# Another emission order for a fused retention and gated MLP kernel

## The chip, the core and the metric

One NeuronCore of a Trainium2 chip runs the whole program in one launch. The metric is the device time in microseconds of that core. The kernel is written against five engines with a queue each: PE (TensorE), DVE (VectorE), ACT (ScalarE), POOL (GpSimd) and SP (SyncE, which here issues nearly all DMA transfers). An engine takes the instructions of its queue in the order in which the program emitted them.

## What is computed

Retention attention over 8 sequences of 576 positions with 8 heads of 64, then a gated MLP with a mix over the positions, and a residual:

```python
scores = (q @ k.T) / sqrt(64)
x = (scores * Dmat) @ v              # Dmat[i,j] = gamma_h**(i-j) for i >= j, else 0; heads side by side: (8, 576, 512)
h = gelu_tanh(x @ w_in)              # (8, 576, 1024)
u, w = h[..., :512], h[..., 512:]
w_n = (w - mean(w)) / sqrt(var(w) + 1e-6) * g_ln
w_s = einsum('ts,bsd->btd', w_sg, w_n) + b_sg[None, :, None]
out = x + (u * w_s) @ w_out
```

## The kernel before, in words

**Tiling.** The sequences go through in 4 pairs (p). A pair has 1152 positions, which are 9 tiles of 128 rows; the middle one is half of each sequence. The attention of a pair is done in 5 blocks (n = 0 to 4) of two tiles, but the middle one (n = 2) of one; block b is 5p + n, tile i is 9p + m. The MLP's position mix is done for each sequence ("batch", 2p + e).

**One block of attention.** SP loads q, k and v (`a_load`, lines 315 and 318). A preparation (`a_prep`) scales q and v by powers of gamma (line 361) and casts k (351; 349 on ACT); it is done by POOL, for block 0 by DVE and ACT too. q and k are transposed by PE (`a_T`, 398) and copied out by DVE (`a_Tev`, 413), or, from block 10 on, by a transposing DMA of SP (`a_TX`, 418). `a_S` (449) makes the scores, `a_Sev` on DVE masks them (462, 465). `a_Z` (485), `a_Zsum` (510, 513) and `a_Zev` (517, 519) keep the running state k.T v. `a_O` and `a_O2` (531) give the output, which ACT copies to the tile xT (`a_Oev`, 588).

**The MLP of a tile.** `m_V` (599) multiplies by the right half of w_in, ACT makes gelu of it (`m_Vg`, 606), DVE the statistics (`m_stats`, 614 and 615), POOL the reciprocal deviation (`m_rs`, four small instructions, 619 to 622) and ACT the normalised rows (`m_norm`, 634, 631). `m_U` (646) and `m_Ug` (656) do the left half. When the five tiles of a batch have been normalised, eight `m_W` (665) mix the positions, and `m_Wg` on DVE (675) gates. `m_O` (696; 691 adds x for the first pair) multiplies by w_out; `m_Oev` (711 on ACT for the first pair, 713 on DVE later, with the residual tile xr, which a transposing DMA, `m_X`, 705, makes from xT) writes the tile ob, and SP stores it (`m_store`, 718). The last tile, 35, is done in two halves.

**At the start.** Both halves of w_in come through two staging tiles (load at 239) and are cast by DVE (246) and ACT (248). Then the same staging tile of the right half takes four fifths of w_sg in two loads (260), so these wait for both casts. w_sg is cast (271), turned by `build_wT` (779) and copied (783). `to_col`, `col_math` and `to_rows` (724, 728 to 738, 745) make columns and rows of g_ln and b_sg; `rows` (749), `place_vmid` (767, 768) and `place_wT` (771, 772) put them into place. A fill (216) is a matmul on zeros that nothing reads; fill n is emitted by the name fn.

**Buffers.** Tiles are taken from rings by tag (`BUFS`): 8 of ld, 2 of ldq, 3 of vb, 2 each of qb, kb, qT and kT, 5 of xr, 4 of ob, 3 of vg. PSUM has a ring of two (pp: transposes, scores, attention outputs) and one of four (d: all the others, fills among them; an `a_Z` takes two, or one). The ring's next tile waits for the readers of the one that had its place.

**What sets the order.** The kernel first makes a list of 925 jobs, each with an engine and a function that emits its instructions; the job's number is its place in that list. `Planner.emit` then goes through the string `ORDER` and calls the functions in that order. Durations, due times and costs in `add(...)` are not used for it. So each engine's queue is the sub-list of its own jobs, in the order of `ORDER`, and the order of two jobs of different engines matters only through what they wait for and through the order in which tiles are taken from a ring.

The jobs that are spoken of by number:

| job | what |
|---|---|
| 0, 1, 2; 6, 7, 8; 12, 13, 14 | `a_load` of q, k, v of blocks 0; 1; 2 |
| 3, 9 | loads of w_in, right and left half |
| 4, 5 | casts of w_in's right half, DVE and ACT |
| 15, 16; 17 | loads of w_sg to the staging tile; its last rows |
| 23, 24, 25; 31, 32 | loads of q, k, v of block 3; k, v of block 4 |
| 72; 75; 76; 77, 79; 78, 80 | `zero_wnat`; `to_col`; `col_math`; `to_rows`; `rows` |
| 81, 82 | `place_vmid`, `place_wT` |
| 103, 104, 106, 107 | block 0: q prepared (DVE), k cast (ACT), `a_T`, `a_Tev` |
| 195, 197; 196, 198 | block 0: `a_S`; `a_Sev` |
| 267; 268, 270; 269, 271; 272, 273; 274, 275 | block 0: `a_Z`; `a_Zsum`; `a_Zev`; `a_O`, `a_O2`; `a_Oev` |
| 187, 188, 189, 190; 192, 193 | block 18: q twice, k, v prepared; block 19: k, v |
| 184; 775 | block 17: v prepared; `m_rs` of tiles 27 and 28 |
| 191, 194 | transposing loads of q, k of blocks 18 and 19 |
| 581, 585, 569, 577 | stores of tiles 15, 16, 13, 14 |
| 659, 667, 740 | `m_X` of tiles 18, 19, 23 |
| 907, 911, 915, 919, 922 | `m_O` of tiles 32, 33, 34, and of 35 in two halves |

Of the kernel before, what the change touches and what calls it, by code (L numbers as in the profile page):

```python
# [17 lines left out]
PR = dict(PB0=10000.0, O=4000.0, PB=9900.0, S=2000.0, S2=400.0, Z=1901.0, V=6000.0, V2=900.0, U=1260.0, W=4000.0, WS=19000.0, slack=60.0, pen=500.0)  # L18

ORDER = (  # L20
# [33 lines left out]
)  # L54


# [1006 lines left out]
```

## Time and profile before

| | |
|---|---|
| three runs | 214.28, 215.05 and 230.25 us |
| their median | 215.05 us |
| span of the profiled execution, first to last instruction | 212.7 us |
| busy in it: PE, DVE, ACT, POOL | 195.4, 147.3, 117.0, 118.4 us |
| mean granted TensorE clock | 0.991 |
| moved by DMA | 50.45 MB, 237 GB/s over the span |

A profile gives one execution; its span leaves out what lies before the first and behind the last instruction, and its time is not recorded apart from the span. In the rows, L and a number is a line of the kernel; "out<-in" are the tiles written and read; a bracket at the end tells how long the engine was idle ahead of the row and which engine's work ended that. SPq is SP issuing a DMA: a row of it is the time of the issue, not of the transfer. "Granted clock" is the share of full speed that TensorE's clock gate gave.

### The profile page before, as it was taken

To read this page: it belongs to the slowest core of one execution; us is meant where nothing else is said; L and a number is where in the kernel's file an instruction comes from. 1 tells how busy PE (TensorE), PEld (TensorE's weight loads), DVE (VectorE), ACT (ScalarE), POOL (GpSimd) and SP (SyncE) were. 2 spreads that over 40 slices of the span, in tenths; PEclk is the share of its full clock that TensorE was granted. 3 is DMA by queue.
4 is the path that set the end of the run, shared out by engine and by line. 5 is a ranking of instruction groups with operands and counts; after the bars stand their busy time and mean duration, and the time that the engine had idled before them with its cause. 6 is when DMAs were issued, how large, how long until landed. Compare 5 with 4: busy or idle time off the path is not lost.

```text
span 212.7 us, 7684 instructions
## 1 busy us (share of the span) xinstructions
PE 195.4 (92%) x3282; PEld 133.8 (63%) x3282; DVE 147.3 (69%) x287; ACT 117.0 (55%) x207; POOL 118.4 (56%) x169
## 2 busy tenths in 40 slices
PE   7796699788899999999999999899999899999992
PEld 5674585665656677765677666666475665666760
DVE  4783787767858489666857387687747686866473
ACT  5228757842785941888463867444642648443400
POOL 8955285979782999752868965008593344112000
PEclk9999969999999999999999999999999999999999
DMA  6999999999999999999999999999999897626755
GB/s 163 335 295 262 169 377 295 287 284 296 271 250 294 277 272 295 137 197 307 339 319 204 222 177 103 223 303 120 338 287 198 191 253 130 197 69 152 245 157 197
DMA packets 94228, 50.45 MB, mean 237 GB/s; under 512 B 45354, under 2 KB 87602, under 8 KB 94194
## 3 DMA queue, kind: packets, MB, share of 16 engines
q1 hardware_dynamic: 94176, 49.97, 101.1%
q8 instruction: 25, 0.41, 0.9%
q14 instruction: 9, 0.07, 0.1%
q10 hardware_dynamic: 18, 0.00, 0.0%
HBM read 32.79 MB, written 9.44 MB: 199 GB/s over the span
## 4 chain that ended last, share of the span: by engine, by line
PE 65%; DMA 14%; SPq 7%; POOL 5%; issue 3%; DVE 3%; ACT 2%; POOLq 0%; ACTq 0%
PE wp L665 16%; PE op L696 13%; PE hu L646 11%; PE hv L599 11%; DMA ld<-in_v_dram 7%; PE pp L531 5%; DMA ld<-in_k_dram 5%; SPq L315 4%; PE pp L449 3%; DMA kT<-kb 2%; POOL vb L361 2%; PE zp L485 2%; PE pp L398 2%; SPq L318 1%; POOL mv L620 1%
## 5 line engine op out<-in xcount | busy, mean ns | idle before, releaser
L361 POOL TENSOR_TENSOR vb<-ld,gpow 128x1024 bf16<-128x1024 f32 (+1 forms) x20 | 34.6, 1733 | 19.8 <-DMA out_dram<-ob 11.1
L462 DVE TENSOR_TENSOR ret<-pp,msk 128x1024 bf16<-128x1024 f32 x32 | 38.6, 1212 | 8.0 <-PE pp L449 7.9
L665 PE MATMUL wp<-wT,vn 128*128 128x288 bf16 x256 | 40.6, 286 | 0.0
L599 PE MATMUL hv<-w_in,xT 128*128 128x512 bf16 x144 | 36.6, 380 | 0.2 <-issue 0.2
L646 PE MATMUL hu<-xT,w_in 128*128 128x256 bf16 (+1 forms) x320 | 36.3, 262 | 0.3 <-DVE uT L675 0.3
L696 PE MATMUL op<-w_out,uT 128*128 128x512 bf16 (+1 forms) x148 | 35.7, 373 | 0.2 <-ACT vg L606 0.2
L614 DVE BATCH_NORM_STATS2 bst<-vg 128x6 f32<-128x512 f32 x36 | 24.6, 684 | 14.9 <-ACT vg L606 14.9
L606 ACT ACTIVATE vg<-hv 128x512 f32<-128x512 f32 x36 | 21.4, 596 | 23.8 <-PE hv L599 18.2
L646 PEld LDWEIGHTS <-w_in 128*128 128x128 bf16 x320 | 28.4, 98 | 7.4 <-issue 0.5
L675 DVE TENSOR_TENSOR uT<-wp,uT 128x288 bf16<-128x288 f32 x64 | 26.6, 448 | 8.1 <-PE wp L665 5.9
L634 ACT ACTIVATE vn<-vg,mv 128x512 bf16<-128x512 f32 x32 | 25.6, 810 | 11.5 <-POOL mv L622 11.3
L656 ACT ACTIVATE uT<-hu 128x512 bf16<-128x512 f32 x36 | 21.1, 593 | 19.3 <-PE hu L646 19.1
L665 PEld LDWEIGHTS <-vn 128*128 128x128 bf16 x256 | 24.1, 98 | 8.1
L361 POOL TENSOR_TENSOR qb<-ldq,gpow 128x1024 bf16<-128x1024 f32 x14 | 26.5, 1904 | 4.3 <-DMA ldq<-in_q_dram 3.8
L588 ACT ACTIVATE xT<-pp 128x512 bf16<-128x512 f32 (+1 forms) x40 | 20.4, 550 | 12.6 <-PE pp L531 12.4
L619 POOL TENSOR_SCALAR mv<-mv 128x2 f32<-128x2 f32 (+1 forms) x20 | 4.5, 226 | 37.0 <-DVE mv L615 25.9
L713 DVE TENSOR_TENSOR ob<-op,xr 128x512 f32<-128x512 f32 (+1 forms) x28 | 18.3, 668 | 9.2 <-PE op L696 7.4
L696 PEld LDWEIGHTS <-uT 128*128 128x128 bf16 x148 | 13.9, 98 | 11.9 <-issue 0.5
L599 PEld LDWEIGHTS <-xT 128*128 128x128 bf16 x144 | 12.8, 98 | 12.7 <-issue 0.5
L665 PE MATMUL wp<-wT,vmid 128*128 128x288 bf16 x64 | 18.4, 287 | 0.0
L351 POOL CAST kb<-ld 128x1024 bf16<-128x1024 f32 x14 | 14.5, 1038 | 3.8 <-DMA ld<-in_k_dram 3.8
L620 POOL TENSOR_TENSOR mv<-mv,mhalf 128x2 f32<-128x2 f32 (+1 forms) x20 | 13.8, 688 | 1.7
(100 smaller groups left out, 249.9 us busy)
## 6 DMA issues: line engine op xcount, KB each, us to landing
out_dram<-ob SPq DMA_DIRECT2D x35, 256.0 KB, 4.0
ld<-in_k_dram SPq DMA_DIRECT2D x16, 512.0 KB, 7.3
ld<-in_v_dram SPq DMA_DIRECT2D x16, 512.0 KB, 7.1
ldq<-in_q_dram SPq DMA_DIRECT2D x7, 1024.0 KB, 6.8
xT<-in_moe_w_sg_dram SPq DMA_DIRECT2D x2, 576.0 KB, 8.0
ld<-in_q_dram SPq DMA_DIRECT2D x2, 512.0 KB, 8.2
xT<-in_moe_w_in_dram SPq DMA_DIRECT2D x1, 1024.0 KB, 8.0
ld<-in_q_dram SPq DMA_DIRECT2D x8, 128.0 KB, 7.5
```

Of the source, the lines that this page charges most:

```text
L361: ve.tensor_tensor(dst, src, g.unsqueeze(len(src.shape) - 1).to_broadcast(list(src.shape)), op=Alu.mult)
L462: ins = nc.vector.tensor_tensor(ret[:].rearrange("p r (k t) -> p (r k) t", k=2), sc[:].rearrange("p r (k t) -> p (r k) t", k=2), (msk2 if ...
L588: nc.scalar.activation(dst, src, Act.Copy)
L599: ins = nc.tensor.matmul(hv[:], xTs[p][:, m, kk, :], w_in[:, kk, F2:], start=(kk == 0), stop=(kk == KK - 1))
L606: unfence(nc.scalar.activation(vgs[i][:], cur.pop(("hv", i))[:], Act.Gelu_apprx_tanh), ("V", i))
L614: nc.vector.bn_stats(bst[:], vgs[i][:])
L634: nc.scalar.activation(vn[:], vg[:], Act.Identity, scale=mv[:, s, 2:3], bias=mv[:, s, 3:4])
L646: ins = nc.tensor.matmul(hu[:, n, :], w_in[:, kk, 128 * c:128 * c + 128], xTs[p][:, m:m + w, kk, :], start=(kk == 0), stop=(kk == KK - 1), ...
L656: unfence(nc.scalar.activation(uTs[p][:, c0:c1, 128 * m:128 * m + 128 * w], cur.pop(("hu", i, half))[:], Act.Gelu_apprx_tanh), ("U", i, half))
L665: ins = nc.tensor.matmul(ps[:], vns[t0 + j][e][:, 128 * c:128 * c + 128], wT[e][j][:, half * HS:(half + 1) * HS], start=(j == 0), stop=(j ...
L675: ins = nc.vector.tensor_tensor(uTs[p][:, c, col:col + HS], cur.pop(("wp", b, c, half))[:], uTs[p][:, c, col:col + HS], op=Alu.mult)
L696: ins = nc.tensor.matmul(op[:], uTs[p][:, c, r], w_out[:, c, cs], start=(p >= XP and c == 0), stop=(c == KK - 1), skip_group_check=True)
```

## The change

The string `ORDER` is replaced by another with the same 925 jobs and the same six fills (4, 5, 6, 6, 10 and 14). Nothing else differs: every job emits the same instructions. The heads of the queues, before and after:

```
PE   before  f4 f6 75 f5 f6 77 79 106 267 197 195 f14 272 273
PE   after   f4 75 f10 f14 77 f6 106 197 195 f6 267 272 273 79
SP   before  0 1 2 3 6 7 8 12 17 16 15 13 14 23 9 24 31 25 34
SP   after   1 0 2 3 6 7 15 17 8 16 12 13 14 23 9 24 31 25 32
DVE  before  72 103 76 78 107 196 4 198 80 268 270 112
DVE  after   76 72 103 78 107 198 4 196 268 80 270 112
ACT  before  104 269 5 274 275 81 271 277 22
ACT  after   104 81 5 269 274 82 275 22 277
```

Of the later queues, a stretch of SP's and of POOL's, and the end of PE's:

```
SP   before  585 667 191 659 194 569 71 675 577 740 662
SP   after   191 194 581 585 569 659 740 667 577 71 662
POOL before  717 183 187 188 189 190 192 775 184 193 796
POOL after   183 187 188 775 190 184 189 192 796 811 193
PE   before  894 907 919 922 911 915
PE   after   904 907 911 915 919 922
```

The diff, cut to the lines that hold these places:

```diff
@@ -18,39 +18,39 @@
 ORDER = (
-    '0 f4 1 2 f6 72 3 73 6 103 75 74 f5 76 7 104 f6 77 79 105 78 106 8 107 267 197 269 195 f14 196 5 12 4 198 108 17 '
-    '80 272 16 268 270 109 273 274 15 13 275 111 81 276 112 279 110 14 201 199 271 277 113 22 289 278 f10 280 23 200 '
-    '21 20 290 202 291 19 9 281 18 24 293 114 82 292 91 286 89 92 294 116 90 31 101 117 87 83 115 287 102 97 88 93 '
-    '296 84 95 295 98 310 94 203 96 99 118 297 204 25 313 298 314 288 300 299 119 316 100 312 315 311 301 85 34 10 11 '
-    '122 302 317 120 123 282 32 318 307 320 86 319 303 36 321 124 308 322 126 304 283 33 305 127 309 121 323 205 207 '
-    '38 206 130 306 352 284 353 208 354 125 35 324 285 355 211 357 212 356 134 332 330 325 26 358 209 374 359 40 210 '
...
-    '781 665 711 657 700 712 579 780 666 583 717 256 713 580 187 719 185 658 581 782 584 718 66 765 186 714 188 70 '
-    '783 257 785 730 784 585 715 731 766 667 722 189 716 738 723 191 190 736 739 726 567 727 737 768 568 192 575 769 '
-    '771 576 767 668 659 772 663 770 194 660 669 775 773 569 258 71 664 792 774 661 184 675 794 793 577 802 795 799 '
-    '845 740 800 803 801 259 804 846 786 805 848 776 662 260 728 670 847 777 261 671 720 262 193 787 724 744 789 721 '
...
-    '910 887 892 898 888 893 891 838 889 918 904 839 899 905 840 896 900 902 897 901 894 903 914 907 895 919 908 922 '
-    '911 909 923 920 924 915 912 921 913 916 917 '
+    'f4 73 1 75 76 74 72 f10 f14 0 104 2 3 6 7 105 103 77 f6 106 78 107 197 195 198 4 81 5 15 17 8 108 109 110 16 '
+    '196 f6 267 268 269 272 273 79 274 80 270 111 276 82 275 22 277 f5 112 201 279 19 280 271 20 18 21 199 289 278 '
+    '202 281 290 291 200 292 93 85 86 94 12 13 14 23 286 113 114 87 293 97 98 88 294 101 102 95 116 117 96 115 9 118 '
+    '119 24 31 296 295 287 89 297 288 298 203 204 83 84 90 300 313 314 301 299 302 99 91 100 315 316 317 92 10 310 '
+    '122 311 307 11 318 120 124 123 319 322 282 320 305 308 309 283 312 126 303 127 306 321 304 323 25 32 33 205 284 '
+    '209 206 121 207 352 34 36 125 128 129 130 134 285 210 353 355 324 339 341 330 208 325 331 340 342 354 357 211 '
...
+    '253 182 183 185 579 738 767 254 186 739 770 580 782 257 187 188 775 69 66 190 68 70 184 189 192 783 583 567 584 '
...
+    '794 805 804 809 847 810 795 796 191 194 581 585 569 659 740 667 792 806 773 730 259 261 797 807 808 811 793 798 '
...
+    '842 843 747 906 914 751 918 898 910 836 844 892 888 889 893 896 894 899 897 895 900 902 903 901 904 905 907 908 '
+    '909 911 912 913 915 916 917 919 922 920 921 923 924 '
 )
```

44 rows, old and new, of the table ORDER are left out of this document.

## The prediction

> **What bounds the kernel now.** I read the page first, then the chain of waits, then the timeline of each queue for the first 60 us, because the two lists differ most there.
>
> ```profile
> span 212.7 us, 7684 instructions
> ...
> PE 195.4 (92%) x3282; PEld 133.8 (63%) x3282; DVE 147.3 (69%) x287; ACT 117.0 (55%) x207; POOL 118.4 (56%) x169
> ...
> GB/s 163 335 295 262 169 377 295 287 284 296 271 250 294 277 272 295 137 197 307 339 319 204 222 177 103 223 303 120 338 287 198 191 253 130 197 69 152 245 157 197
> ```
>
> TensorE is busy for 92% of the span, so after the start whatever it loses is lost at the end too. The transfers run at 250 to 380 GB/s in most of the first 16 slices (5.3 us each).
>
> ```profile
> 7.67 11.30 DMA ld<-in_v_dram
> ...
> 25.67 9.86 DMA ld<-in_k_dram
> 35.58 1.04 POOL kb L351
> ...
> 44.22 0.61 PE wp L665 x5
> ```
>
> The chain of waits (start, length, what) says who sets the pace of the start: two loads, 21 of the first 36 us, then a cast on POOL, and only from the first m_W at 44 us mostly TensorE. So there are two stages: loads until about 45 us, TensorE after it.
>
> ```profile
> 0.00:10.00 10.00, 7.83 (x64) 6.16 (x65) 6.08 (x30) 4.18 (x5) 8.66 (x32) 1.00 0.86 241
> 10.00:20.00 10.00, 8.30 (x190) 5.87 (x191) 6.51 (x8) 4.97 (x9) 5.11 (x4) 1.00 1.18 274
> 20.00:30.00 10.00, 7.22 (x140) 6.04 (x140) 7.32 (x15) 7.65 (x14) 5.08 (x9) 0.91 1.00 265
> 30.00:40.00 10.00, 9.88 (x178) 6.93 (x177) 7.43 (x16) 6.14 (x13) 7.54 (x10) 0.92 1.13 305
> 40.00:50.00 10.00, 7.31 (x201) 5.38 (x201) 6.67 (x8) 5.77 (x10) 8.18 (x8) 1.00 1.18 278
> ```
>
> By stretches (stretch, length, busy PE, PEld, DVE, ACT, POOL, granted clock, DMA share, GB/s): TensorE is idle for 9.5 of the 50 us, most of all at 20 to 30 and at 40 to 50, and the granted clock falls to 0.91 and 0.92 where TensorE was thin.
>
> **The change part by part.** No work is added or removed; every engine gets the same jobs in another order. I take the places where an order makes its engine wait.
>
> *The fills.* Ahead of the first transposes, a_T(0,q), TensorE had fills of 4, 6, 5 and 6; it now has 4, 10, 14 and 6, the 10 and 14 behind to_col and ahead of to_rows(0).
>
> ```profile
> 1.24 3.88 PE L216 MATMUL scr<-warm 128*128 128x256 f32 x10 [1.24 <-DVE warm L175]
> 6.03 0.20 PE L724 MATMUL tp<-identf,rsrc 9*128 9x9 f32 x1 [0.91 <-DMA rsrc<-in_moe_b_sg_dram]
> ...
> 8.74 0.66 PE L745 MATMUL tp<-ident,col 128*4 128x128 bf16 x9
> 9.33 0.64 PE L398 MATMUL pp<-ident,qb 64*128 64x64 bf16 x32
> ...
> 11.87 3.29 PE L216 MATMUL scr<-warm 128*128 128x256 f32 x14
> ```
>
> The fills of 10 and 14 are 24 records. At 11.87 one costs 0.235 us, at the start 0.388. All fast is 5.6 us, all slow 9.3. TensorE now idles from about 3 to 6.0 waiting for rsrc, so I take ten slow and 14 fast: 3.9 + 3.3 = 7.2, from 6.2 to 13.4. to_rows(0) (0.4 of the 0.66) and the six records of the next fill (1.4) follow: a_T(0,q) starts at 15.2 and not at 9.33, 5.9 later (4 to 8).
>
> *The load of w_sg on SP.* Job 15 was at place 11 of SP's queue and is at 7, ahead of a_load(1,v). It writes the staging tile that the casts of w_in (jobs 4 on DVE, 5 on ACT) read, so SP waits there for both, with every later load behind it.
>
> ```profile
> 8.56 0.17 DVE L738 TENSOR_TENSOR col<-colr,col 128x10 bf16<-128x10 f32 x1
> 9.16 0.41 DVE L749 COPY row4b<-tp 4x512 bf16<-4x512 bf16 x1 [0.42 <-PE tp L745]
> 10.02 1.23 DVE L413 COPY qT<-pp 128x2048 bf16<-128x2048 bf16 x1 [0.45 <-PE pp L398]
> 12.06 1.23 DVE L462 TENSOR_TENSOR ret<-pp,msk 128x1024 bf16<-128x1024 f32 x1 [0.82 <-PE pp L449]
> 13.20 0.68 DVE L246 CAST w_in<-xT 128x1024 bf16<-128x1024 f32 x1
> ```
>
> On DVE the cast still stands behind the first masking of scores. From a_T at 9.33 to the end of that cast were 4.55 us; nothing in between changes, so it ends at 15.2 + 4.6 = 19.8.
>
> ```profile
> 11.66 1.05 ACT L248 ACTIVATE w_in<-xT 128x1024 bf16<-128x1024 f32 x1
> ...
> 17.37 0.63 ACT L767 ACTIVATE vmid<-row4b 4x512 bf16<-4x512 bf16 x1
> ```
>
> On ACT place_vmid (four of 0.63, 2.5 us) now comes first and needs to_rows(0) and rows(0), about 14.3: 16.8, and the cast ends at 17.9. DVE is the later one.
>
> ```profile
> 5.89 1.74 SPq L315 DMA_DIRECT2D ld<-in_k_dram  x1
> 7.67 3.56 SPq L315 DMA_DIRECT2D ld<-in_v_dram  x1
> ...
> 25.67 3.35 SPq L315 DMA_DIRECT2D ld<-in_k_dram  x2
> ```
>
> SP comes to this place at 7.6 and stands until 19.8. Behind it are a_load(1,v), issued at 7.67 before, and all later loads. Asked for by then are 3.7 MB (by their shapes five loads of 0.52 and half of w_in, 1.05), which the first three slices (0.87 + 1.78 + part of 1.57) move by 14. From there until about 2 us past 19.8 the transfers have nothing to do. The ten loads up to and with a_load(3,k), place 16 in both lists, are 5.3 MB; at the mean of the slices 3 to 7, 280 GB/s, 18.8 us: they land at about 40.6, and the k cast of block 3, at 35.58 before, starts some 5 us later (3 to 7). The Trainium skill ("DMA: Bandwidth & Descriptors", on the anatomy of one DMA) says that DMA engines do not wait on semaphores, and that the issuing sequencer does so ahead of the dispatch. By that rule one waiting load holds all behind it, as taken here; SP's rows agree in that they follow one another and never overlap, and no run here shows the blocked load yet.
>
> *What of it reaches the end.* Of the 5 us two parts are given back. The new TensorE order puts 0.75 us more work ahead of the first m_W (the scores of block 4 among it, by their places in the lists). And of the 2.7 us that TensorE idled at 40 to 50, a part is a wait that would now lie beside the later loads; but this is not:
>
> ```profile
> PE 65%; DMA 14%; SPq 7%; POOL 5%; issue 3%; DVE 3%; ACT 2%; POOLq 0%; ACTq 0%
> ```
>
> ```profile
> 47.42 1.28 issue
> ...
> 54.29 0.88 issue
> ```
>
> The first line is the chain's share by engine. The two pieces called issue wait for nothing that the profile shows and need not go with the order. That leaves 1.4, half of which I count: 5 - 0.75 - 0.7 = 3.5 us. Bounds: 0.5, if other TensorE work lies ready throughout, and 6. Cover for the rest there is none: after 60 us TensorE has hardly any idle time.
>
> *The clock.* TensorE has even less to do between 22 and 30 us. The rows of 0.91 and 0.92 are a loss of 1.7 us of full clock; the same once more would be 1.7 at most, partly beside waits for loads: +0.5 (0 to 1.7). The Trainium skill ("TensorE: Matmul & The Clock Gate", Part 1) has the clock at half after an idle window of some 3.4 us, until a busy one. By that rule the thin stretch would cost two windows more, 3.4 us, and not 0.5, and the sum would be 2.9 higher; this trace has only the two rows above to set beside it.
>
> *Lead of the m_W groups.* A group needs the gelu, statistics, POOL's m_rs and two or more m_norm of the last m_V.
>
> ```profile
> 64.30 0.97 PE hv L599 x4
> ...
> 74.67 2.45 PE wp L665 x20
> ...
> 191.84 0.86 PE hv L599 x4
> ...
> 198.78 2.45 PE wp L665 x20
> ```
>
> Before, 10.4 us lay between the last m_V and the group of batch 1, and 6.9 for batch 7, with no gap. Counting the TensorE jobs between them in the new list at their lengths (0.86 for an m_V, m_U or m_O, 0.61 for an m_W, the small ones at theirs), batch 1 gets about 6.9, batch 4 7.4, batch 5 6.7. That is the least that went well before, three times over: +1 (0 to 3).
>
> *SP around 165 us.* The transposing load kT of blocks 18 and 19 now stands ahead of three stores and the residual transposes of tiles 18, 23 and 19; its cast on POOL moves behind m_rs(27) and a cast of v.
>
> ```profile
> 163.88 2.45 SPq L418 DMA_TRANSPOSE kT<-kb  x1
> ...
> 169.96 1.22 SPq L705 DMA_TRANSPOSE xr<-xT  x1
> ...
> xr<-xT SPq DMA_TRANSPOSE x27, 3.7
> ```
>
> m_X(23) was issued at 169.96; behind the later kT, 2.45, three stores and one more m_X, I have it about 7 us later, while its m_O moves ahead. With 3.7 us to land it comes a little after that m_O, and m_Oev(23) then holds DVE's queue, and with it the m_Wg of batch 6 and TensorE's four PSUM buffers: +1 (0 to 4).
>
> *The tail.* Last are now the two half stores of tile 35, and not a whole one.
>
> ```profile
> 208.90 0.69 DVE L713 TENSOR_TENSOR ob<-op,xr 128x512 f32<-128x512 f32 x1 [0.17 <-PE op L696]
> ...
> out_dram<-ob SPq DMA_DIRECT2D x35, 256.0 KB, 4.0
> ...
> out_dram<-ob SPq DMA_DIRECT2D x2, 128.0 KB, 1.8
> ```
>
> After DVE's last row 3.1 us are left. A small store saves 1.3 of them, but the last whole one is only about 0.9 earlier: -0.8 (0 to -1.3).
>
> **Sum.** 212.7 + 3.5 + 0.5 + 1 + 1 - 0.8 = 217.9 us of span. The runs shown are 214.28, 215.05 and 230.25; their median is 2.35 above the span, so 220.2: I say 220. All low ends together give 214.3, all high ones 229.8.
>
> **The rivals.** *The start is absorbed.* The loads are late, but TensorE finds other work, and by 60 us it is where it was. For it: 9.5 us of its first 50 are idle. Against it: the k cast that the chain goes through depends on the late loads. The start then costs 0.5, and the time is 217.2; below about 2.6 us of start term the change is within 2%. This is not slower by what a measurement tells.
>
> *Faster.* The gaps called issue (3% of the span, 6 us) fall for two thirds elsewhere, beside waits; the start is absorbed, and the terms of 1 are nothing: 212.7 - 4 + 0.5 - 0.8 + 2.35 = 210.7. Against it: nothing in the new lists shortens anything there.
>
> *The clock stays down.* Thin TensorE work made the rows of 0.91 and 0.92, together 1.7 us lost; two more such stretches are 3.4 in place of 0.5, so 223. (This is what the rule of the clock page would make of it.) For it: TensorE waits for loads at 22 to 30. Against it: what it then does slowly is in part waiting anyway.
>
> **How the numbers follow.** Forecast, slower at about 220: 0.45; the clock rival, also slower: 0.10; start absorbed, 211 to 219: 0.35; faster: 0.10. A measurement tells about 2% from no change, 210.7 to 219.4. So faster by over 2% has 0.10, within 2% 0.35, slower 0.55. The range, 212.5 to 226, leaves out the faster case and the part of the slower ones where the bounds add up; the slower cases alone are 219.4 to 226.
>
> **What would show it.** In the changed profile: fills of 24 records between 6 and 13.5 us; a gap of about 12 us in SP's rows ahead of w_sg's load; thin transfers at 14 to 21; the first cast of k for block 3 near 41; the first m_W near 48. If SP issues w_sg's load before 12 us, or the first m_W comes before 46, the start term is wrong. If m_V of batches 1, 4 and 5 are followed by their m_W with no gap, the lead term is nothing; if DVE does not wait for xr around 180 us, the SP term is.

## The result and the profile after

The changed kernel takes 221.85 us (median of 4 runs, 220.34 to 222.24); the kernel before took 216.21 us in the same session. The ratio is 1.033 (95% interval 1.028 to 1.039): slower by 3.3% (the two medians are 2.6% apart). The profiled execution took 221.47 us, with a span of 219.8 us against 212.7 before. All ratios below are over the kernel before, run on the same chip in the same session, and leave out disturbed executions; the medians beside them are over all runs. The kernels ran in four sessions, so medians from two of them are best compared by their ratios.

The page of the changed kernel:

```profile
span 219.8 us, 7655 instructions
...
PEclk9999999999999999999999999999999699999999
...
GB/s 170 337 162 13 323 187 371 284 289 340 219 274 260 226 272 350 197 181 178 261 343 274 163 186 313 206 133 96 199 364 230 161 228 212 197 124 256 187 162 255
```

The fourth slice (16.5 to 22 us) is the first thing to see: 13 GB/s where the kernel before moved 262. The one slow digit of the TensorE clock, in slice 6 before, now stands in slice 32.

The stretches (stretch, length, busy PE, PEld, DVE, ACT, POOL, granted clock, DMA share, GB/s):

```profile
10.00:20.00 10.00, 8.68 (x96) 6.69 (x95) 4.89 (x5) 3.46 (x5) 3.70 (x3) 1.00 0.49 126
20.00:30.00 10.00, 6.97 (x189) 4.62 (x189) 6.39 (x10) 6.49 (x13) 1.90 (x1) 1.00 0.93 238
30.00:40.00 10.00, 8.88 (x172) 5.63 (x174) 8.72 (x21) 5.13 (x10) 7.33 (x9) 1.00 1.02 299
...
170.00:180.00 10.00, 8.91 (x147) 6.89 (x149) 4.54 (x11) 5.99 (x13) 4.47 (x10) 0.83 1.11 205
```

From 10 to 20 us TensorE looks busier than before (8.68 for 8.30), but much of that is fills: up to 11.8 us they follow one another at 0.43 us, after it at 0.22.

SP's queue, then the chain of waits:

```profile
5.79 1.74 SPq L315 DMA_DIRECT2D ld<-in_k_dram  x1
20.50 0.37 SPq L260 DMA_DIRECT2D xT<-in_moe_w_sg_dram  x1
```

```profile
6.28 8.12 PE scr L216 x24
...
19.87 0.60 DVE w_in L246
...
32.64 11.08 DMA ld<-in_k_dram
...
43.77 1.05 POOL kb L351
...
49.01 2.56 PE wp L665 x20
```

SP issues nothing for 13 us, until the cast of w_in on DVE ends (19.87 + 0.60). The chain begins with the 24 fills, where before it began with loads, and passes the first m_W at 49.0 instead of 44.2. (Its cast of k at 43.77 is that of block 4; block 3's is at 42.41.)

The second place is near 168 us. Before, SP issued the load of k of block 17 ahead of two residual transposes, and that of q of block 18 (ldq) right behind them; now four such transposes stand ahead of both. SP before, then after:

```profile
141.29 1.72 SPq L318 DMA_DIRECT2D ld<-in_k_dram  x2
143.06 2.62 SPq L705 DMA_TRANSPOSE xr<-xT  x2
145.73 1.31 SPq L315 DMA_DIRECT2D ldq<-in_q_dram  x1
```

```profile
145.31 5.75 SPq L705 DMA_TRANSPOSE xr<-xT  x4
151.12 1.79 SPq L318 DMA_DIRECT2D ld<-in_k_dram  x2
...
154.32 0.62 SPq L315 DMA_DIRECT2D ldq<-in_q_dram  x1
```

POOL's casts for blocks 17 and 18 after the change, then TensorE, which waits for them:

```profile
157.59 1.04 POOL L361 TENSOR_TENSOR qb<-ld,gpow 128x512 bf16<-128x512 f32 x1 [5.17 <-DMA ld<-in_q_dram]
...
161.82 3.76 POOL L361 TENSOR_TENSOR qb<-ldq,gpow 128x1024 bf16<-128x1024 f32 x2 [2.63 <-DMA ldq<-in_q_dram]
...
167.30 2.91 POOL L361 TENSOR_TENSOR vb<-ld,gpow 128x1024 bf16<-128x1024 f32 x2
170.33 1.04 POOL L351 CAST kb<-ld 128x1024 bf16<-128x1024 f32 x1
```

```profile
170.26 0.22 PE L485 MATMUL zp<-vb,qb 64*64 64x64 bf16 x3 [1.38 <-POOL vb L361]
...
171.42 0.45 PE L485 MATMUL zp<-vb,kb 64*64 64x64 bf16 x32 [0.73 <-POOL kb L351]
...
171.90 4.46 PE L646 MATMUL hu<-xT,w_in 128*128 128x256 bf16 x32
```

The third is the end, on SP, DVE and TensorE:

```profile
207.81 4.19 SPq L705 DMA_TRANSPOSE xr<-xT  x3
212.05 5.18 SPq L718 DMA_DIRECT2D out_dram<-ob  x8
```

```profile
212.07 0.69 DVE L713 TENSOR_TENSOR ob<-op,xr 128x512 f32<-128x512 f32 x1 [2.39 <-DMA xr<-xT]
...
214.45 2.20 DVE L713 TENSOR_TENSOR ob<-op,xr 128x512 f32<-128x512 f32 x4 [0.36 <-DMA out_dram<-ob]
```

```profile
212.81 2.86 PE L696 MATMUL op<-w_out,uT 128*128 128x512 bf16 x16 [0.68 <-DVE ob L713]
```

m_Oev(31) waits for its transposed residual, the second of three that SP issues from 207.8 on, and eight stores stand behind them.

**One table for all runs.** The two lists order TensorE's work differently, so jobs cannot be compared one to one. I add up the lengths of TensorE's jobs (the planner's) in each list and compare the moments at which both have done the same amount. The difference is the lag, good to about half a microsecond. The columns are times of the kernel before; "end" is the difference of the spans.

| profiled run | 59 | 102 | 132 | 153 | 164 | 170 | 201 | end |
|---|---|---|---|---|---|---|---|---|
| after | 2.7 | 5.0 | 4.1 | 2.2 | 2.9 | 6.0 | 5.8 | 7.1 |
| e1_sp_late_wsg | 3.1 | 4.5 | 4.1 | 2.2 | 2.6 | 6.3 | 6.1 | 7.4 |
| e2_fills_later | 5.4 | 7.5 | 6.6 | 4.7 | 5.1 | 10.0 | 9.8 | 10.6 |
| e3_casts_first | -0.1 | -0.1 | -0.9 | -2.9 | -1.9 | 0.9 | 1.1 | 3.1 |
| e4_loads_ahead | 4.5 | 6.0 | 5.1 | 3.2 | 6.0 | 5.6 | 5.5 | 6.6 |
| e5_sp_start | 0.5 | 1.7 | 0.8 | -1.1 | -0.5 | 5.9 | 5.8 | 6.7 |
| e6_loads_in_gap | 3.9 | 4.5 | 3.6 | 7.4 | 7.7 | 7.4 | 7.2 | 8.3 |
| e7_tail_order | 4.8 | 6.1 | 5.3 | 3.3 | 4.1 | 7.0 | 7.1 | 7.9 |
| e8_three_mended | 1.3 | 1.3 | 0.5 | 5.6 | 5.9 | 5.5 | 5.4 | 5.7 |
| e9_transposes_in_gap | 1.3 | 3.1 | 2.2 | 0.3 | 2.9 | 2.5 | 2.3 | 3.1 |
| e10_four_mended | 0.5 | 1.9 | 1.3 | -0.6 | 1.7 | 1.3 | 1.1 | 1.5 |
| e11_before_wsg | 0.9 | 3.4 | 2.5 | 4.0 | 4.0 | 3.9 | 4.8 | 4.7 |
| e12_before_wsg_fills | 6.4 | 6.3 | 5.6 | 6.3 | 6.3 | 6.2 | 6.3 | 6.3 |

A row is one execution, and some are far from their kernel's others: e1's took 221.82 us (the three others 217.96 to 219.85), e2's 224.97 (218.76 to 220.55), and e9's, 217.50, was the fastest of six.

For the changed kernel it reads: 5 us lost by 102 us, 2.8 won back by 153, 3.1 lost at 164 to 170, 1.3 at the end. Not all of the 5 is the start: the pieces called issue fall on both sides. The kernel before has such pieces of 1.28 and 0.88 at 47 and 54 and 0.37 at 62; the changed kernel of 0.98 at 52, 1.03 and 0.93 at 64 and 73, and 0.45 and 0.27 near 101. Without them the start costs 3.9 us by either column, 59 or 102.

### The profile page after: what moved, and what is told of

The parts are those of the page before. It is cut to its first block, busy times and chain, and to the rows that moved or that the text cites. A ratio compares the mean times of both kernels' runs of the same rounds, so it can differ in the third digit from the quotient of the medians.

```text
span 219.8 us, 7655 instructions
## 1 busy us (share of the span) xinstructions
PE 196.4 (89%) x3253; PEld 134.9 (61%) x3282; DVE 148.1 (67%) x287; ACT 117.1 (53%) x207; POOL 118.1 (54%) x169
## 4 chain that ended last, share of the span: by engine, by line
PE 67%; DMA 11%; DVE 7%; SPq 4%; issue 3%; ACT 3%; POOL 2%; DVEq 0%; ACTq 0%; POOLq 0%
PE wp L665 15%; PE hu L646 13%; PE op L696 10%; PE hv L599 10%; DMA ld<-in_k_dram 8%; PE pp L531 5%; PE scr L216 4%; PE pp L449 4%; DVE ret L462 2%; PE zp L485 2%; SPq L318 2%; DMA rsrc<-in_moe_b_sg_dram 2%; PE pp L398 2%; DVE bst L614 1%; DMA out_dram<-ob 1%
## 5 line engine op out<-in xcount | busy, mean ns | idle before, releaser
L665 PE MATMUL wp<-wT,vn 128*128 128x288 bf16 x256 | 40.9, 286 | 0.1
L646 PE MATMUL hu<-xT,w_in 128*128 128x256 bf16 (+1 forms) x320 | 38.0, 270 | 0.0
L599 PE MATMUL hv<-w_in,xT 128*128 128x512 bf16 x127 | 35.1, 380 | 1.2 <-issue 0.3
L675 DVE TENSOR_TENSOR uT<-wp,uT 128x288 bf16<-128x288 f32 x64 | 27.4, 451 | 12.8 <-PE wp L665 10.8
L696 PE MATMUL op<-w_out,uT 128*128 128x512 bf16 (+1 forms) x136 | 34.0, 373 | 1.4 <-DVE ob L713 0.7
L646 PEld LDWEIGHTS <-w_in 128*128 128x128 bf16 x320 | 29.0, 101 | 6.7 <-ACT w_in L248 0.2
L599 PEld LDWEIGHTS <-xT 128*128 128x128 bf16 x144 | 13.3, 98 | 11.8 <-ACT xT L588 0.3
L216 PE MATMUL scr<-warm 128*128 128x256 f32 (+1 forms) x46 | 14.6, 478 | 1.2 <-DVE warm L175 1.2
```

The source lines that it names most:

```text
L216: nc.tensor.matmul(scr[:, :w], warm[:, :128], warm[:, :w], start=True, stop=True, skip_group_check=True)
L599: ins = nc.tensor.matmul(hv[:], xTs[p][:, m, kk, :], w_in[:, kk, F2:], start=(kk == 0), stop=(kk == KK - 1))
L646: ins = nc.tensor.matmul(hu[:, n, :], w_in[:, kk, 128 * c:128 * c + 128], xTs[p][:, m:m + w, kk, :], start=(kk == 0), stop=(kk == KK - 1), ...
L665: ins = nc.tensor.matmul(ps[:], vns[t0 + j][e][:, 128 * c:128 * c + 128], wT[e][j][:, half * HS:(half + 1) * HS], start=(j == 0), stop=(j ...
L675: ins = nc.vector.tensor_tensor(uTs[p][:, c, col:col + HS], cur.pop(("wp", b, c, half))[:], uTs[p][:, c, col:col + HS], op=Alu.mult)
L696: ins = nc.tensor.matmul(op[:], uTs[p][:, c, r], w_out[:, c, cs], start=(p >= XP and c == 0), stop=(c == KK - 1), skip_group_check=True)
```

## The experiments

Theory A is the prediction's: SP's standing still for the casts makes the start late, and the fills make the casts late. Its rivals are B (the fills alone), and C (what is won at the start is lost again). Theories D, E and F came from the trace after: D, late loads cause the step near 168 us; E, the clock there does; F, SP's last jobs cause the late end. Where the expectations name 43.8 us for the k cast of block 3, I had taken the row of block 4; block 3's is at 42.41.

**e1_sp_late_wsg**

```
SP - 1 0 2 3 6 7 15 17 8 16 12 13 14
   + 1 0 2 3 6 7 8 16 12 17 15 13 14
```

> The changed kernel with one edit: on SP the loads of w_sg (job 15) and of its last rows (17) go back behind a_load(2,q), as before; the fills stay at 10 and 14. Theory A (SP's wait for the casts of w_in is what makes the start late): no gap in SP's rows between 7.5 and 20 us, no empty slice of the transfers, the k cast of block 3 at 36 to 38 and not at 43.8, the first m_W near 46 and not at 49.0, and the time 2 to 3 us below the changed kernel's: about 219.3. Theory B (the 24 fills ahead of to_rows(0) make it late, by TensorE's own first transposes at 16.1): the first m_W stays past 48 and the time within 1 us of 221.9. Theory C (what is won at the start is lost again between 60 and 75 us, where the changed kernel fell back by 1.5 us more): the first m_W earlier, the time still about 221.5.

Measured: 219.53 us, ratio 1.022 (1.012 to 1.031). The edit left w_sg's other half (16) ahead, and SP stood for it from 11.2 to 18.7 us, so the step was not tested. The lag at 102 is 4.5, in the longest of its four executions. The ratio, which leaves that one out, is 1.1% below the changed kernel's, so a part of the gain may be there, but no trace shows it: this run tells little.

**e2_fills_later**

```
PE - f4 75 f10 f14 77 f6 106 197 195 f6 267 ... 87 293
   + f4 75 77 f6 106 197 195 f14 f6 267 ... 87 f10 293
```

> The changed kernel with one edit: on TensorE the fills of 10 and 14 go back to about where they stood before, the 14 behind a_S(0,0) and the 10 ahead of a_O(1); SP keeps w_sg's load at its place 7. Theory A (SP's wait counts, and it ends with the cast on DVE that stands behind a_T(0,q)): a_T(0,q) at about 9 us, the cast of w_in ends near 13.5, SP issues w_sg's load near 14 and not at 20.5, so about two thirds of the loss at the start goes: first m_W 46 to 47, time 219 to 220. Theory C (lost again between 60 and 75 us): time about 221.5. If the fills also kept the granted clock up, the rows of 10 to 30 us would show less than 1.00.

Measured: 220.50 us, ratio 1.026 (1.016 to 1.036). SP issued w_sg's load at 16.68, 3.8 us earlier, yet the lag at 102 is 7.5. The row that answers for it, on TensorE:

```profile
30.30 4.63 PE L217 MATMUL scr<-warm 128*128 128x256 f32 x10 [0.68 <-DVE zb L514]
```

Ten fills took 0.46 us each, twice the 0.235 of a full clock, with real work waiting behind them. This execution had a granted clock of 0.68 from 30 to 40 us and took 4.4 to 6.2 us more than the three others, which have no trace; their ratio is below the changed kernel's, but not clear of it. The experiment does not tell A from C.

**e3_casts_first**

```
DVE - 76 72 103 78 107 198 4      ACT - 104 81 5
    + 76 72 103 4 78 107 198          + 104 5 81
```

> The changed kernel with one edit: the two casts of w_in (job 4 on DVE, job 5 on ACT) go ahead of the jobs that wait for TensorE's to_rows(0), so they start when their load has landed (11.3 us). SP's list and the fills stay as changed: w_sg's load is still at place 7. Theory A: SP issues it near 12.6 and not at 20.5; the transfers pause little; the k cast of block 3 at 37 to 39, the first m_W near 46.5, the time about 219.5, as where SP's list itself is mended. Theory B (fills): first m_W past 48, time within 1 us of 221.9. That place 7 in itself costs something, whatever it waits for: between the two.

Measured: 217.57 us, ratio 1.015 (1.008 to 1.022), 4.3 us below the changed kernel's median, some 3.9 by the ratios. SP, with the same list, got through 8 us earlier:

```profile
12.52 0.37 SPq L261 DMA_DIRECT2D xT<-in_moe_w_sg_dram  x1
```

The lag at 102 is -0.1. Neither SP's list nor a fill was touched, so B falls: the same fills cost nothing here. C falls too. For A it leaves one rival, that TensorE needs the casts of w_in themselves earlier; e5 answers it. The k cast of block 3, expected at 37 to 39, still came at 40.93, so that mark is not what the start is lost by in the new list. The step near 168 is there too, with nothing of the clock in it (1.00 from 170 to 180):

```profile
167.01 0.22 PE L486 MATMUL zp<-vb,qb 64*64 64x64 bf16 x3 [2.96 <-POOL vb L362]
```

**e4_loads_ahead**

```
SP - 178 586 181 578 566 582 574 65 64 67 508
   + 178 586 181 65 64 67 578 566 582 574 508
```

> The changed kernel with one edit: on SP the loads of k and q of block 17 and of q of block 18 (jobs 65, 64, 67) go ahead of four residual transposes that no one needs before 158 us (m_X of tiles 15, 13, 16, 14; 5.75 us of SP). Theory D (TensorE's step back of 2.5 to 3 us at 168 to 172 us comes from these loads: late q casts on POOL, therefore late v of block 17 and late k of block 18): the q cast of block 17 starts near 152 and not at 157.6, v of block 17 is ready before 168, a_Z(17) does not wait 1.4 us, and the time is 2 to 3 us lower, about 219.3. Theory E (the granted clock of 0.83 at 170 to 180 us is the cause by itself): time within 0.7 us of 221.9, and 0.83 still there. If the chain of slots for loads only moves the wait elsewhere: a gain of about 1 us.

Measured: 220.50 us, ratio 1.029 (1.019 to 1.038). The step from 164 to 170 is gone (-0.4), and another of 2.8 stands between 153 and 164. My expectation had these transposes needed by no one before 158 us. They read the attention output of the second pair, in one of the two xT buffers, and ScalarE wants that buffer for the fourth:

```profile
158.89 1.09 ACT L589 ACTIVATE xT<-pp 128x512 bf16<-128x512 f32 x2 [3.76 <-DMA xr<-xT]
```

**e5_sp_start**

```
SP - 1 0 2 3 6 7 15 17 8 16 12 13 14
   + 1 0 2 3 6 7 8 12 17 16 15 13 14
```

> The changed kernel with SP's first 13 jobs as before but for the first two (a_load(1,v), a_load(2,q) and w_sg's last rows ahead of both halves of w_sg, jobs 16 and 15). The run e1_sp_late_wsg had left job 16 at place 8, so SP still waited there from 11.2 to 18.7 us and that run did not test the step. Fills and casts stay as changed: the cast of w_in on DVE still ends at 19 to 20. Theory A (the loads that stand behind w_sg cost the start): here only a_load(1,v), a_load(2,q) and the last rows get ahead, SP still stands until about 19 for job 16, so three loads of 1.2 MB are won: k cast of block 3 at about 41, a gain of 1 to 2 us, 220 to 221. Theory B (the fills alone): no gain, 221.9. If the mended casts (e3_casts_first, 217.6) are the whole story, this kernel must stay well above 218.

Measured: 219.21 us, ratio 1.020 (1.012 to 1.028). With three more loads issued ahead of the stand, the lag at 102 falls to 1.7; fills and casts are as changed, so B falls a second time, and so does the rival that e3 left. A holds: what counts is which loads stand behind w_sg's, and for how long. SP's rows, the stand now from 14.9 to 19.35:

```profile
13.80 1.11 SPq L264 DMA_DIRECT2D ld<-in_moe_w_sg_dram  x1
19.35 2.15 SPq L260 DMA_DIRECT2D xT<-in_moe_w_sg_dram  x2
```

**e6_loads_in_gap**

```
SP - 178 586 181 578 566 582 574 65 64 67 508 496 589 504 69 66 68 70
   + 65 64 67 178 586 181 578 566 582 574 69 66 68 70 508 496 589 504
```

> The changed kernel with two edits on SP: the loads of k and q of block 17 and q of block 18 (65, 64, 67) go ahead of qT(15), where SP stands idle for 2.7 us in the changed kernel and where their slots are long free; the loads of v of blocks 18 and 17 and of k of blocks 18 and 19 (69, 66, 68, 70) go ahead of four stores. Unlike e4_loads_ahead this hardly moves the four residual transposes, whose delay made ScalarE wait 3.8 us for its buffer there. Theory D (late loads make the step back of 2.5 to 4 us near 168 us): no wait ahead of a_Z(17) over 0.5 us and no new one between 156 and 164; time 218.5 to 219.5. Theory E (the clock of 0.83 at 170 to 180): within 0.7 us of 221.9. In e3_casts_first the step was there at a granted clock of 1.00, so I expect D.

Measured: 222.50 us, ratio 1.032 (1.024 to 1.041): no gain. Again the step at 164 to 170 is gone (-0.3), and 3.8 us are lost before 153. On SP, then TensorE:

```profile
140.51 5.58 SPq L418 DMA_TRANSPOSE qT<-qb  x1
146.14 1.26 SPq L705 DMA_TRANSPOSE xr<-xT  x1
147.50 3.12 SPq L418 DMA_TRANSPOSE kT<-kb  x1
```

```profile
152.52 0.64 PE L449 MATMUL pp<-qT,kT 64*64 64x128 bf16 x32 [4.00 <-DMA kT<-kb]
```

Behind the three loads qT(15) held SP for 5.58 us (3.35 in the changed kernel), and kT(15) came too late for a_S(15).

**e7_tail_order**

```
SP - 747 906 914 751 918 898 910 836 844 901 909 913 917 921 924
   + 747 898 906 751 836 910 914 844 918 901 909 913 917 921 924
```

> The changed kernel with SP's last 15 jobs in another order: the residual transpose of tile 31 first and the stores of tiles 28 and 30 ahead of the transposes of tiles 33, 34 and 35; all else as changed. Theory F (the end is late because m_Oev(31) waits 2.4 us for its transpose, which stands behind three others, and the last results wait for stores that stand behind them too): DVE has no wait over 0.6 us after 207 us, TensorE runs through to its last m_O, and the time is 1.3 to 2 us lower, 219.9 to 220.5. Rival (the stores' own bytes set the end: 7 stores in the last 8 us whatever the order): within 0.5 us of 221.9.

Measured: 222.56 us, ratio 1.030 (1.022 to 1.038). The total shows no gain; the executions range from 219.90 to 225.13, and the profiled one, 222.33, lagged 6.1 at 102 with the very same start. The end itself is better:

```profile
211.37 0.69 DVE L713 TENSOR_TENSOR ob<-op,xr 128x512 f32<-128x512 f32 x1 [0.41 <-PE op L696]
...
216.87 0.76 DVE L713 TENSOR_TENSOR ob<-op,xr 128x256 f32<-128x256 f32 x2 [0.99 <-DMA out_dram<-ob]
```

m_Oev(31) no longer waits for its residual. From 201 us to the end the lag grows by 0.8 and not 1.3; over the eight profiled runs with the changed tail it grows by 1.2 in the mean, over the three with this one by 0.5. F holds in the mean, at half the size that I expected; that is near what the table can resolve, and the total does not show it.

**e8_three_mended** has the edits of e3, e6 and e7.

> The changed kernel with the edits of e3_casts_first, e6_loads_in_gap and e7_tail_order together. If the three places (start, loads of blocks 17 and 18, tail) are what makes the change slower, and their costs add: 221.9 - 4.3 - 3 - 1.6 = 213, which is below the kernel before (215.4 on the last chip) by about 1 per cent, as the changed order wins some 2 to 3 us between 60 and 155 us. If they overlap: 215 to 217. If the stretch between 60 and 155 us gains nothing once the start is on time: 215.

Measured: 221.17 us, ratio 1.013 (1.003 to 1.023). Start mended (1.3 at 102), end mended, and e6's own wait for kT(15), 5.1 us here, eats it.

**e9_transposes_in_gap**

```
SP - 178 586 181 578 566 582 574 65 64 67 508
   + 586 578 178 181 65 64 67 566 582 574 508
```

> The changed kernel with one edit on SP: the residual transposes of tiles 17 and 15 (m_X, 1.3 us each) go into the 2.7 us in which SP stands idle ahead of qT(15), where their slots are free; kT(15) follows qT(15) at once, then the loads of k and q of block 17 and q of block 18, then the three other transposes. e6_loads_in_gap had put the loads into the gap; there qT(15) then took 5.3 us of SP and kT(15) came 5 us late for a_S(15). Theory D (the late loads of blocks 17 and 18 make TensorE step back near 168 us): the loads are issued 7 us earlier, at 144 to 148; no wait ahead of a_S(15) and none over 0.5 us ahead of a_Z(17); TensorE's lag behind the kernel before does not grow by more than 0.5 us between 144 and 180 us (it grew by 3.0); time about 219. If transposes and loads, which share SP and the transfer engines, simply cannot all come in time here, a wait turns up elsewhere between 144 and 172 us and the time is 221 to 222.

Measured: 220.44 us, ratio 1.020 (1.012 to 1.027). In its fastest execution the step at 164 to 170 is gone (-0.4), a_S(15) does not wait, and the wait for the residual transposes is back, on ACT and then on TensorE:

```profile
155.72 1.08 ACT L588 ACTIVATE xT<-pp 128x512 bf16<-128x512 f32 x2 [3.52 <-DMA xr<-xT]
```

```profile
156.37 1.04 PE L599 MATMUL hv<-w_in,xT 128*128 128x512 bf16 x3 [2.08 <-ACT xT L588]
```

**e10_four_mended** has the edits of e3, e5, e7 and e9.

> The changed kernel with the casts of w_in first (as in e3_casts_first), SP's first 13 jobs as in e5_sp_start, the edit of e9_transposes_in_gap and the tail of e7_tail_order. If the costs of start, middle loads and tail add: start about 4, middle 3, tail 0.9, so 221.9 - 8 = 214, at or below the kernel before (216 on these chips). If e9_transposes_in_gap only moves its wait: 216.5 to 217.5, as e3_casts_first less the tail.

Measured: 216.73 us, ratio 1.011 (1.005 to 1.018): 5.1 us below the changed kernel's median, some 4.7 by the ratios, the fastest of the changed lists, and still not faster than the kernel before. By the table the start's 1.9 and the 2.3 from 153 to 164 (ScalarE's wait for a residual transpose, 3.25 us here) are what it lacks.

**e11_before_wsg** is the kernel before with one edit.

```
SP - 0 1 2 3 6 7 8 12 17 16 15 13 14
   + 0 1 2 3 6 7 15 17 8 12 16 13 14
```

> The kernel BEFORE with one edit: w_sg's load (15) and its last rows (17) at places 7 and 8 of SP's list, ahead of a_load(1,v), as in the changed kernel; fills, casts and all other engines as before, so the second cast of w_in ends at 13.9 and not at 20.5. My working (the cost is SP's standing still until that cast ends): SP stands from 7.6 to 13.9, about when the transfers run out of what they were given, so little is lost: 0 to 1 us. Rival (place 7 is bad by itself, whenever the casts end): the 4 us of the start, 219 to 220.

Measured: 218.22 us, ratio 1.011 (1.002 to 1.020): about 2 us where I expected 0 to 1, though the interval, 0.3 to 4.3 us, reaches that far. SP stood until 15.71. The price came by another load than the one that I had followed, a_load(1,v), right behind the stand; on TensorE:

```profile
24.96 0.64 PE L485 MATMUL zp<-vb,qb 64*64 64x64 bf16 x32 [4.01 <-POOL vb L361]
25.53 4.63 PE L216 MATMUL scr<-warm 128*128 128x256 f32 x10
```

Part of the price is the clock: all six executions have a mean granted clock of 0.976 to 0.984, the eleven of the kernel before in the same session 0.992 to 1.000.

**e12_before_wsg_fills** is e11 with the changed fills.

```
PE - f4 f6 75 f5 f6 77 79 106 267 197 195 f14 272 273 111 276 279 ... f10 293
   + f4 75 f10 f14 77 79 f6 106 267 197 195 f6 272 273 111 276 f5 279 ... 293
```

> The kernel BEFORE with the edit of e11_before_wsg and the fills of 10 and 14 ahead of to_rows(0), 6 and 5 as in the changed kernel: place 7 and late casts together. My working: a_T(0,q) at 15 to 16, the cast on DVE ends near 20, SP stands from 7.6 until then, an empty slice of transfers near 16 to 21; the first m_W near 48 and the time 3 to 5 us above the kernel before. Rival (the middle of the new list, not the start, made it slower): within 1.5 us of the kernel before.

Measured: 222.51 us, ratio 1.038 (1.031 to 1.044): with nothing of the new middle and end, the old list becomes as slow as the new one. SP's row, and the page's line:

```profile
19.45 0.37 SPq L260 DMA_DIRECT2D xT<-in_moe_w_sg_dram  x1
```

```profile
GB/s 167 336 168 73 252 202 350 291 280 282 293 295 251 306 253 246 309 163 240 330 330 267 165 271 122 167 179 254 264 301 242 168 204 193 183 53 168 243 166 192
```

The lag is 6.4 at 59 us and 6.3 at the end: what the start loses, nothing later gives back. Place 7 and late casts together cost over three times what place 7 does alone. Here too the clock has a share:

```profile
20.00:30.00 10.00, 7.09 (x135) 4.67 (x135) 5.54 (x10) 5.55 (x10) 2.95 (x2) 0.83 1.03 234
30.00:40.00 10.00, 6.94 (x134) 5.37 (x135) 6.50 (x14) 5.73 (x10) 5.99 (x8) 0.83 1.15 296
```

That is 3.4 us of full clock lost, where the kernel before has 1.7. The fills alone, with w_sg's load at its old place in the old list, were not run, so in that list the two cannot be told apart.

## Why the prediction was right, and where it was not

The forecast, slower, at about 220 us of 212.5 to 226, was right in sign and close in size: 221.85. Its sum had a span of 217.9; the span came out at 219.8, and only 1.7 us lay around it and not 2.35.

**Fills and load, +3.5: right.** The fills took 8.12 us (7.2 forecast: 13 of the 24 ran at the slow pace, not ten), SP's stand ended at 20.5 (19.8), a slice of the transfers was empty, the k cast of block 3 started at 42.4 (41), the first m_W at 49.0 (48). The five profiled runs with this start lag by 5.0, 6.0, 4.5, 6.1 and 3.1 at 102 us, mean 4.9; the four with the stand ended early or put off (e3, e5, e8, e10) by 1.2; e1, whose other half of w_sg kept its place, and e2 are left out. That makes 3.7 us, beside the 3.9 worked out above. e3 and e5 show the cause in the new list, and e12 that the start alone is enough. The Trainium skill ("DMA: Bandwidth & Descriptors", on the anatomy of one DMA) has the wait on the issuing sequencer; the trace agrees, with 13 us without a row on SP, and 8 fewer when the cast came 8 us earlier. My way from there to the end, by the k cast of block 3, was too narrow: e3 won all of it back with that cast at 40.9.

**Clock, +0.5: nothing in the profiled executions.** They have 0.991 and 0.992, one slow stretch each; it only moved, from 20 to 40 us to 170 to 180. Of the changed kernel's four executions two have 0.992 (221.47 and 222.23 us) and two 0.981 and 0.982 (220.34 and 222.24), so the mean clock does not sort its totals. But e4 and e7, with the same start, show 0.83 and 0.66 from 30 to 40, so a start like this risks up to 3.4 us of full clock (0.34 of 10 us) in one execution, and none in another; the kernel before lost 1.7 there. By the rule of the Trainium skill ("TensorE: Matmul & The Clock Gate", Part 1) an idle window of some 3.4 us halves the clock. e11 agrees: 4.01 us idle, then ten fills at 0.46 us. Near 171 us two waits of 1.38 and 0.73 with little work between them were enough: the 32 matmuls behind them took 4.46 us, where in e3 the same took 2.81, although e3 had waited longer there (2.96 and 0.55 us). So the length of a wait alone does not tell whether the clock falls. That the start would cost two such windows, and the time be 223, did not come about in the profiled run; in e12 the start did cost two.

**Lead of the m_W groups, +1: nothing.** The lag does not grow at the first m_W of batches 1, 4 and 5, and TensorE has no gap ahead of them.

**SP around 165 us, +1 (0 to 4): the place right, size and mechanism wrong.** It cost 3.1. m_X(23) was issued 8.4 us later, at 178.34 (forecast: about 7), but the named wait, m_Oev(23) for xr, isn't there: in the group of m_Oev,

```profile
L713 DVE TENSOR_TENSOR ob<-op,xr 128x512 f32<-128x512 f32 (+1 forms) x28 | 18.3, 669 | 8.4 <-DMA xr<-xT 3.7
```

3.7 us in all are waits for xr; 2.39 are the one at 212.07, and the rest is at 203. The step of the prediction that failed is the one that followed the later kT, the stores and m_X(23) and nothing ahead of them. The loads of q and k of block 17 and q of block 18 stand earlier in the same list, behind four residual transposes (145.3 to 151.1). POOL therefore stood 5.17 and 2.63 us, and v of block 17 and k of block 18 came late. The five kernels with these loads ahead (e4, e6, e8, e9, e10) have no step there. In the six with SP's middle as changed it is 2.8 to 6.4: 2.8 in e3 with a full clock in that stretch, so theory E falls as its cause, and the most in e5 and e2, where the clock's digit there is 5, which fits a clock that makes it larger. But each of my three orders paid 2.3 to 5.1 us at another wait on the same queue. Whether a fourth would be free of it stays open; it wasn't tried.

**The tail, -0.8: wrong in sign, +1.3.** I priced the last two half stores and not the order ahead of them. The prediction's step "the last whole one is only about 0.9 earlier" took for granted that m_Oev would have its residual.

**Not forecast: a gain.** From 132 to 153 us the new list wins 1.9 to 2.0 us in each run in which no load stands ahead of qT(15) (all but e6 and e8). The sums of six stretches of 5 us, before from 125 on and after from 129 on (sum, then busy PE and the others):

```profile
sum 30.00, PE 28.39 PEld 19.15 DVE 22.82 ACT 16.50 POOL 13.09; mean PE 4.73 PEld 3.19 DVE 3.80 ACT 2.75 POOL 2.18
```

```profile
sum 30.00, PE 29.62 PEld 20.73 DVE 24.41 ACT 17.99 POOL 16.15; mean PE 4.94 PEld 3.45 DVE 4.07 ACT 3.00 POOL 2.69
```

1.2 us of it is idle time that TensorE no longer has; the rest I cannot tell from the planner's lengths. So the total came out near the forecast partly because two errors met: the late places cost 3.1 + 1.3 where I had +0.2 for both, and the lead term and the middle took 2.9 back.

## What to carry to other kernels

In an order written by hand, look on each queue for the first instruction that waits for another engine, and price what stands behind it by how long it waits, not by its place: in the new list the same place cost some 4 us or nothing, by when the casts ended, and in the old one about 2. A step moved to free one wait pays on the same queue: before you move a transfer ahead, write down the latest time of each job that it passes, among them who wants the buffer that it reads. And judge a repair at the place it mends: the totals of one kernel here often differ by 2 us and more from one execution to the next.

## What the runs showed of the hardware

Two things I had not expected. A transpose on SP is not a short issue: over the runs with the changed list qT took from 1.70 us (e7) to 6.14 us (e5) of SP's queue; the longest stood right behind loads of k, while a residual transpose took 1.2 to 1.3 in the median and at most 4.36 (e3). And DVE and POOL can hinder each other when both read tiles in SBUF. In e11, on DVE and on POOL,

```profile
13.38 2.30 DVE L246 CAST w_in<-xT 128x1024 bf16<-128x1024 f32 x1
```

```profile
13.23 1.90 POOL L361 TENSOR_TENSOR qb<-ld,gpow 128x1024 bf16<-128x1024 f32 x1 [2.43 <-DMA ld<-in_q_dram]
```

the cast of w_in took 2.30 us where it takes 0.68 otherwise, and ended only after POOL's operation, which had started 0.15 us ahead of it. It held SP for 1.6 us more. In the kernel before the same cast started first, at 13.20, and took 0.68, and POOL's operation the longer time:

```profile
13.31 2.33 POOL L361 TENSOR_TENSOR qb<-ld,gpow 128x1024 bf16<-128x1024 f32 x1 [2.48 <-DVE ret L462]
```

It is not so for all work: the masking of scores beside that operation, which reads PSUM, took its usual 1.22 us.
